# Two decode layers on one core: the last w2 in products of 512 columns, and x moved as its 16 real rows

## The chip, the cores and the metric

The kernel runs on one NeuronCore of a Trainium2 chip. The time is the device time of one execution in microseconds; the time before is the median of three runs. A profile is one more execution, taken by the hardware profiler.

## The reference

Two layers of the same weights, each a grouped-query attention with a cache and a gated feed-forward, for a batch of four single tokens. The part that matters:

```python
# B = 4, D = 512, 32 query heads, 8 kv heads, 4096 cached keys, Dh = 128, F = 1792, all float32
def _B_ref(x, w1, w3, w2):
    gate = jnp.einsum("bsd,df->bsf", x, w1)
    up = jnp.einsum("bsd,df->bsf", x, w3)
    h = _silu(gate) * up
    return jnp.einsum("bsf,fd->bsd", h, w2)

x = x + _A_ref(_layernorm(x), k_cache, v_cache, wq, wo)
x = x + _B_ref(_layernorm(x), w1, w3, w2)
# the same two lines once more: the second layer
```

The result is the last `x`, 4 rows of 512 numbers.

## The kernel before

**Loads.** All large arrays go through one buffer, `space`, of 216 units of 128 KB. The list `LOADS` names every load and its place, in the order in which they are issued on SyncE's queue. `pump` (L129 to L148) issues the next load as soon as its place is free in the program's order, and `done` (L153) frees a place after the last product that reads it and calls `pump` again. Before the first layer `x` is loaded on ScalarE's queue into `x_sb` (L161).

**The layout of x.** The 4 x 512 numbers stand in a 128 x 128 tile: column block k of 128 columns lies on partitions 32k to 32k+3, and the other 112 partitions are zeros. The host builds that tile for the input and takes the rows out of it for the output. `same` and the layer norm (`deviation`, `layernorm`) work on this layout.

**The accumulator bank.** `sums_ps` is one PSUM tile of 128 x 512. `x_ps` is its first 128 columns, `misc` its second 128, and `wide` all 512. The program is a tile framework's with a manual schedule: the order within each engine is the order of the code, and the framework puts in the semaphores.

**The feed-forward.** The w1 products (L473) fill `pg`; ScalarE takes the sigmoid (L478) and VectorE multiplies (L480). Then come the w3 products in two parts (`up`, L467), between them the residual: one product of the identity with `x_sb` starts the sum in `x_ps` (L517). `hidden` (L485) multiplies gate and up parts, `turn_h` turns the result into `hT`, in which chunk m of 128 hidden values is 128 partitions x 4 columns (L491, and L495 to L497 for the second part). `down` (L506 to L514) goes through the 14 chunks of w2: for each of the four column blocks k one product of `hT[:, m, :]` (the stationary side, 4 columns) with 128 columns of w2 is added to partitions 32k to 32k+3 of `x_ps`. After chunk 1 the second part of `hT` is turned.

In the last layer the w2 chunks come in five loads, of 4, 4, 3, 2 and 1 chunks. After the last chunk VectorE copies `x_ps` to `x_sb` (L579), and SyncE stores the 128 x 128 tile to `out` (L580).

Of the kernel before, what the change touches and what calls it, by code (L numbers as in the profile page):

```python
# [8 lines left out]
F32 = mybir.dt.float32  # L9
AF = mybir.ActivationFunctionType  # L10
# [3 lines left out]
B, D, HQ, HKV, SK, DH, F = 4, 512, 32, 8, 4096, 128, 1792  # L14
LAYERS = 2
REP = HQ // HKV
P = 128
KC = D // P
# [64 lines left out]
def tile_decode_layers(ctx: ExitStack, tc: tile.TileContext, x, kv, wqo, w1, w3, w2, out):  # L83
    nc = tc.nc
    ctx.enter_context(tc.manual_schedule())
    const = ctx.enter_context(tc.tile_pool(name="const", bufs=1))
    work = ctx.enter_context(tc.tile_pool(name="work", bufs=2))
# [5 lines left out]
    def place(at, n):  # L93
        return space[:, at * KB:(at + n) * KB]
# [34 lines left out]
    def pump():  # L129
        while state["next"] < len(LOADS):  # L130
            at, src, keys = entry(*LOADS[state["next"]])
            n = sum(size for _, size in keys)
            if any(taken[at:at + n]):
                return
            taken[at:at + n] = [True] * n
            dst = place(at, n)
            if src is None:
                for i in range(3):
                    nc.scalar.activation(dst[:, i * BLOCK:(i + 1) * BLOCK], stored[i], AF.Copy)
                nc.sync.dma_start(dst[:, 3 * BLOCK:], kv[TURN][:, 3 * BLOCK:2 * U])  # L140
            else:
                nc.sync.dma_start(dst, src)
            for key, size in keys:
                where[key] = at, size
                if key[:3] == ("kv", 0, TURN) and key[3] in KEPT:
                    where[("kv", 1, TURN, key[3])] = at, size
                at += size
            state["next"] += 1  # L148

    def loaded(*key):  # L150
        return place(*where[key])

    def done(layer, *key):  # L153
        if layer == 0 and (key[0] in ("wq", "wo") and key[1] >= HELD or key[:3] == ("kv", 0, TURN) and key[3] in KEPT):
            return
        at, n = where[key]
        taken[at:at + n] = [False] * n
        pump()

    x_sb = const.tile([P, P], F32, name="x_sb")  # L160
    nc.scalar.dma_start(x_sb, x)  # L161
    pump()


    ident = const.tile([P, P], F32, name="ident")
# [29 lines left out]
    hT = const.tile([P, 14, B], F32, name="hT")  # L195
    sums_ps = psum.tile([P, KC, P], F32, name="sums_ps")
    nc.vector.memset(sums_ps, 0.0)
    x_ps, misc = sums_ps[:, 0, :], sums_ps[:, 1, :]
    wide = sums_ps.rearrange("p k c -> p (k c)")
# [8 lines left out]
    def turned():  # L208
        return psum.tile([P, 4, P], F32, name="turned", tag="turned")


    def busy(n):
        if n:
            pt = scores().rearrange("p (k c) -> p k c", k=KC)
            nc.tensor.matmul(pt[:, 0:n, :], ident, ident.unsqueeze(1).to_broadcast([P, n, P]),
                             start=True, stop=True)
# [139 lines left out]
    def exponent(i, ps, acc, scale=None):  # L356
        p = work.tile([P, NT, P], F32, name="p", bufs=1)
        nc.scalar.activation(p.rearrange("p n s -> p (n s)"), ps, AF.Exp, bias=acc[:, i:i + 1],  # L358
                             scale=1.0 if scale is None else scale, accum_out=acc[:, 2 + i:3 + i])
        return p  # L360
# [97 lines left out]
    def feed_forward(layer, xT, rstd, factor):  # L458
        pg = o_ps[0]
        sides = o_ps[1], pg  # L460
        w1_sb = place(0, CORE).rearrange("p (k f) -> p k f", k=KC)

        def up(u, ks):
            for k in ks:
                w = loaded("w3", layer, KC * u + k)
                for j in range(4):
                    nc.tensor.matmul(sides[u][32 * j:32 * j + 32, 0:FW[u]], xT[:, 32 * k:32 * k + 32],  # L467
                                     w[:, j * FW[u]:(j + 1) * FW[u]], start=(k == 0), stop=(k == KC - 1))
                done(layer, "w3", layer, KC * u + k)

        for k in range(KC):
            for j in range(4):
                nc.tensor.matmul(pg[32 * j:32 * j + 32, 0:FJ], xT[:, 32 * k:32 * k + 32],  # L473
                                 w1_sb[:, k, j * FJ:(j + 1) * FJ], start=(k == 0), stop=(k == KC - 1))
            if k == 0:
                factor()
        gate = work.tile([P, FJ], F32, name="gate", tag="p", bufs=1)
        nc.scalar.activation(gate, pg[:, 0:FJ], AF.Sigmoid, scale=rstd[:, 0:1])  # L478
        nc.scalar.activation(spare, half[:, 0:1], AF.Exp)
        nc.vector.scalar_tensor_tensor(gate, pg[:, 0:FJ], rstd[:, 0:1], gate, op0=ALU.mult, op1=ALU.mult)  # L480
        pt = turned()

        def hidden(u):
            s = slice(FW[0] * u, FW[0] * u + FW[u])
            nc.vector.scalar_tensor_tensor(gate[:, s], sides[u][:, 0:FW[u]], rstd[:, 0:1], gate[:, s], op0=ALU.mult, op1=ALU.mult)  # L485

        def turn_h(u):
            if u == 0:
                busy(BUSY[3] if layer < LAYERS - 1 else 0)
                for i in range(2):  # L490
                    nc.tensor.transpose(pt[:, i, :], gate[:, i * P:(i + 1) * P], ident)  # L491
                nc.vector.tensor_copy(hT[:, 0:8, :],
                                      pt[:, 0:2, :].rearrange("p i (j b) -> p (i j) b", j=4)[:, :, 0:B])
            else:
                nc.tensor.transpose(pt[:, 2, :], gate[:, 2 * P:3 * P], ident)  # L495
                nc.tensor.transpose(pt[:, 3, :], gate[:, FJ - P:FJ], ident)
                nc.tensor.transpose(pt[0:64, 3, :], gate[:, FJ - 64:FJ], ident)  # L497
                nc.vector.tensor_copy(hT[:, 8:12, :],
                                      pt[:, 2, :].rearrange("p (j b) -> p j b", j=4)[:, :, 0:B])
                last = pt[:, 3, :].rearrange("p (j u b) -> p j u b", j=2, u=2)  # L500
                for i in range(2):
                    nc.vector.tensor_copy(hT[64 * i:64 * i + 64, 12:14, :],
                                          last[64 * i:64 * i + 64, :, i, 0:B])
            busy(BUSY[4] if layer < LAYERS - 1 else 0)

        def down():  # L506
            for m in range(14):
                t = loaded("w2", layer, m)
                for k in range(KC):
                    nc.tensor.matmul(x_ps[32 * k:32 * k + B, :], hT[:, m, :], t[:, k * P:(k + 1) * P],  # L510
                                     start=False, stop=(m == 13))
                done(layer, "w2", layer, m)
                if m == 1:
                    turn_h(1)  # L514

        up(0, range(KC))
        nc.tensor.matmul(x_ps, ident, x_sb, start=True, stop=False)  # L517
        hidden(0)
        up(1, (0, 1))
        turn_h(0)  # L520
        up(1, (2, 3))
        hidden(1)
        down()

    for layer in range(LAYERS):
# [14 lines left out]
        for n, (g, (first, last)) in enumerate(order):  # L540
# [6 lines left out]
            p = exponent(0, ps, acc, scale)  # L547
# [11 lines left out]
            p = exponent(1, ps, acc, scale)  # L559
# [16 lines left out]
        busy(BUSY[2])  # L576
        xT, rstd, factor = layernorm(rowsum)
        feed_forward(layer, xT, rstd, factor)
    nc.vector.tensor_copy(x_sb, x_ps)  # L579
    nc.sync.dma_start(out, x_sb)  # L580


# [43 lines left out]
```

## Time and profile before

| | |
|---|---|
| median of 3 runs | 705.6 us (705.35 to 705.66) |
| the profiled execution's own time | 705.49 us |
| its span | 703.7 us |
| TensorE busy (products) | 420.6 us, 60% |
| VectorE busy | 145.5 us, 21% |
| ScalarE busy | 41.8 us, 6% |
| data moved | 299.18 MB at a mean of 425 GB/s |
| w2 products, both layers (L510) | 224 records, 8.6 us busy |

The span runs from the first to the last instruction of the program; the execution's own time holds what lies around it as well. In the profile PE is TensorE's products and PEld its weight loads, DVE is VectorE, ACT ScalarE, POOL GpSimd, SP SyncE; a trailing q is the engine's instruction queue, which issues the loads. A row reads: line, engine, operation, result <- operands by the program's names, and the sizes as partitions x elements. An f32 product shows as two records, each with a weight load of its own.

### The profile page before, as it was taken

How to read it: one execution, taken by the hardware profiler on the slowest of the kernel's cores; microseconds unless marked ns; L12 is line 12 of the kernel's file. 1: busy time of each engine (PE TensorE's matmuls, PEld its weight loads, DVE VectorE, ACT ScalarE, POOL GpSimd, SP SyncE). 2: the span in 40 equal slices, each digit the busy share in tenths (PEclk: the TensorE clock that was granted, in tenths of full speed). 3: DMA queues.
4: the chain of work that ended last, by engine and by line, in shares of the span. 5: the costliest groups of instructions: out<-in, count | busy, mean ns of one | idle time of the engine just before them, and what ended most of it. 6: DMA issues, size and time to landing. Idle time of an engine off the chain costs nothing.

```text
span 703.7 us, 7223 instructions
## 1 busy us (share of the span) xinstructions
PE 420.6 (60%) x3162; PEld 131.4 (19%) x3162; DVE 145.5 (21%) x507; ACT 41.8 (6%) x99; POOL 3.1 (0%) x10
## 2 busy tenths in 40 slices
PE   2515634753765485486678984474554645656786
PEld 1101111211221121131124221121111211111223
DVE  3102102120130212232131322022111121212231
ACT  0000000100100000010111110010000001000011
POOL 0000000000000000000000000000000000000000
PEclk9967777875996787798899997697778878788889
DMA  9999999999999999999999999999999999999997
GB/s 417 421 414 423 465 421 425 420 460 422 416 456 427 419 443 447 402 432 430 421 416 390 422 446 433 440 418 427 449 443 426 418 434 443 428 429 421 425 420 295
DMA packets 12271, 299.18 MB, mean 425 GB/s; under 512 B 1360, under 2 KB 1616, under 8 KB 4048
## 3 DMA queue, kind: packets, MB, share of 16 engines
q1 hardware_dynamic: 12096, 298.65, 99.1%
q8 instruction: 25, 0.41, 0.2%
q10 hardware_dynamic: 144, 0.07, 0.0%
q14 instruction: 6, 0.05, 0.0%
HBM read 298.65 MB, written 0.07 MB: 424 GB/s over the span
## 4 chain that ended last, share of the span: by engine, by line
DMA 69%; PE 26%; another core or an unknown queue 2%; DVE 1%; ACT 1%; issue 1%; SPq 0%; ACTq 0%; DVEq 0%
DMA space<-in_kv 54%; PE scores L340 10%; PE o L401 10%; DMA space<-in_wqo 8%; DMA space<-in_w 6%; PE turned L365 1%; PE sums_ps L324 1%; ACT p L358 1%; DVE acc L352 1%; PE o L467 1%; PE stored L267 1%; PE stored L445 0%; DVE pT L367 0%; PE sums_ps L313 0%
## 5 line engine op out<-in xcount | busy, mean ns | idle before, releaser
L340 PE MATMUL scores<-space,qT 128*32 128x512 f32 x1024 | 166.0, 715 | 115.9 <-DMA space<-in_kv 115.4
L401 PE MATMUL o<-space,pT 128*16 128x512 f32 x1024 | 152.0, 726 | 112.2 <-DMA space<-in_kv 104.4
L401 PEld LDWEIGHTS o<-space,pT 128*16 128x16 f32 x1024 | 31.2, 110 | 216.7 <-DMA space<-in_kv 118.9
L340 PEld LDWEIGHTS scores<-space,qT 128*32 128x32 f32 x1024 | 35.0, 122 | 190.0 <-issue 185.3
L367 DVE COPY pT<-turned 128x256 f32<-128x256 f32 x32 | 13.6, 425 | 222.4 <-PE turned L365 222.4
L358 ACT ACTIVATE p<-scores,acc 128x512 f32<-128x512 f32 x30 | 20.6, 687 | 566.4 <-DVE acc L352 441.3
L352 DVE TENSOR_REDUCE acc<-scores 128x1 f32<-128x512 f32 x32 | 22.1, 691 | 122.3 <-PE scores L340 122.3
L414 DVE SCALAR_TENSOR_TENSOR o<-o,acc,o 128x128 f32<-128x128 f32 x112 | 39.3, 351 | 17.0 <-PE o L401 13.6
L313 PE MATMUL sums_ps<-space,xT 128*32 128x512 f32 x120 | 18.2, 684 | 20.8 <-DMA space<-in_wqo 20.8
L365 PE MATMUL turned<-ident,p 128*128 128x128 f32 x128 | 22.4, 300 | 12.7 <-ACT p L358 12.7
L425 DVE COPY oT<-sums_ps 128x16 f32<-128x16 f32 x16 | 2.8, 174 | 127.3 <-PE sums_ps L424 127.3
L365 PEld LDWEIGHTS turned<-ident,p 128*128 128x128 f32 x128 | 14.3, 148 | 44.4 <-ACT p L358 22.8
L324 PEld LDWEIGHTS sums_ps<-same,shares 128*128 128x128 f32 x120 | 15.9, 206 | 14.4 <-DVE shares L319 11.9
L324 PE MATMUL sums_ps<-same,shares 128*128 128x4 f32 x120 | 17.2, 266 | 1.0 <-DVE shares L319 1.0
L445 PE MATMUL stored<-space,oT 128*32 128x512 f32 x104 | 13.6, 596 | 0.0
L319 DVE TENSOR_SCALAR shares<-sums_ps,rstd 128x512 f32<-128x512 f32 x15 | 11.1, 743 | 1.8 <-PE sums_ps L313 1.8
L510 PE MATMUL sums_ps<-space,hT 128*4 128x128 f32 x224 | 8.6, 272 | 3.9 <-DMA space<-in_w 3.8
L424 PEld LDWEIGHTS sums_ps<-head,o 128*128 128x128 f32 x32 | 6.2, 242 | 22.1 <-issue 16.7
L467 PE MATMUL o<-space,xT 128*32 128x192 f32 (+1 forms) x128 | 8.7, 403 | 2.3 <-DMA space<-in_w 2.3
L313 PEld LDWEIGHTS sums_ps<-space,xT 128*32 128x32 f32 x120 | 3.3, 113 | 30.6 <-DMA space<-in_wqo 25.1
L424 PE MATMUL sums_ps<-head,o 128*128 128x16 f32 x32 | 7.8, 322 | 1.2 <-DVE o L414 1.2
L473 PE MATMUL o<-space,xT 128*32 128x448 f32 x64 | 6.8, 545 | 2.0 <-DMA space<-in_w 1.3
(102 smaller groups left out, 143.8 us busy)
## 6 DMA issues: line engine op xcount, KB each, us to landing
space<-in_kv SPq DMA_DIRECT2D x9, 4096.0 KB, 24.3
space<-in_wqo SPq DMA_DIRECT2D x4, 4096.0 KB, 29.9
space<-in_kv SPq DMA_DIRECT2D x2, 4608.0 KB, 19.8
space<-in_kv SPq DMA_DIRECT2D x3, 3072.0 KB, 28.4
space<-in_kv SPq DMA_DIRECT2D x8, 1024.0 KB, 8.7
space<-in_kv SPq DMA_DIRECT2D x1, 7168.0 KB, 29.1
space<-in_kv SPq DMA_DIRECT2D x1, 5632.0 KB, 22.9
space<-in_kv SPq DMA_DIRECT2D x3, 1536.0 KB, 12.2
```

What stands on the lines that cost most here:

```text
L313: nc.tensor.matmul(wide[32 * k:32 * k + 32, :], xT[:, 32 * k:32 * k + 32], w[:, k, :], start=True, stop=True)
L324: nc.tensor.matmul(misc[:, h * B:(h + 1) * B], shares[:, h * DH:(h + 1) * DH], same[:, 0:B], start=True, stop=True)
L340: nc.tensor.matmul(ps[32 * b:32 * b + 32, :], qT[:, b, at:at + 32], t[:, i * BLOCK:(i + 1) * BLOCK], start=(m < 2), stop=(m >= TILES - 2))
L352: nc.vector.tensor_reduce(acc[:, i:i + 1], ps, axis=AX.X, op=ALU.max, negate=True)
L358: nc.scalar.activation(p.rearrange("p n s -> p (n s)"), ps, AF.Exp, bias=acc[:, i:i + 1], scale=1.0 if scale is None else scale, accum_out ...
L365: nc.tensor.transpose(pt[:, n, :], p[:, n, :], ident)
L367: nc.vector.tensor_copy(pT, pt.rearrange("p n (b r) -> p n b r", b=B)[:, :, :, 0:ROW])
L401: nc.tensor.matmul(o_ps[i][32 * b:32 * b + ROW, :], pT[:, r // 2, b, :], t[:, j * NB * DH:(j + 1) * NB * DH], start=(r < 2), stop=(r >= TI ...
L414: nc.vector.scalar_tensor_tensor(o, o_ps[s][:, j * DH:(j + 1) * DH], acc[:, 16 + NB * s + j:17 + NB * s + j], o, op0=ALU.mult, op1=ALU.add)
L424: nc.tensor.matmul(misc[:, 0:B * REP], o, head, start=True, stop=True)
L445: nc.tensor.matmul(bank[32 * h:32 * h + 32, :], oT[:, h, :], w[:, h, :], start=first, stop=last)
L467: nc.tensor.matmul(sides[u][32 * j:32 * j + 32, 0:FW[u]], xT[:, 32 * k:32 * k + 32], w[:, j * FW[u]:(j + 1) * FW[u]], start=(k == 0), stop ...
```

## The change

In the last layer the w2 chunk is one product of all 512 columns, into partitions 0 to 3 of `wide`; the residual is brought there by four products with 4 columns of the identity each. The result then stands as 4 rows of 512. VectorE copies the first half of the columns and ScalarE the second half into a 4 x 512 tile `y`, which is stored as 4 rows of 2 KB. The first layer's `down` is as before. On the input side `x` comes as 4 x 512; `x_sb` is set to zero by VectorE and then filled by four loads of 4 rows each on ScalarE's queue.

```diff
     x_sb = const.tile([P, P], F32, name="x_sb")
-    nc.scalar.dma_start(x_sb, x)
+    nc.vector.memset(x_sb, 0.0)
+    for k in range(KC):
+        nc.scalar.dma_start(x_sb[32 * k:32 * k + B, :], x[:, k * P:(k + 1) * P])
     pump()
...
                 t = loaded("w2", layer, m)
-                for k in range(KC):
-                    nc.tensor.matmul(x_ps[32 * k:32 * k + B, :], hT[:, m, :], t[:, k * P:(k + 1) * P],
-                                     start=False, stop=(m == 13))
+                if layer == LAYERS - 1:
+                    nc.tensor.matmul(wide[0:B, :], hT[:, m, :], t, start=False, stop=(m == 13))
+                else:
+                    for k in range(KC):
+                        nc.tensor.matmul(x_ps[32 * k:32 * k + B, :], hT[:, m, :], t[:, k * P:(k + 1) * P],
+                                         start=False, stop=(m == 13))
                 done(layer, "w2", layer, m)
...
         up(0, range(KC))
-        nc.tensor.matmul(x_ps, ident, x_sb, start=True, stop=False)
+        if layer == LAYERS - 1:
+            for k in range(KC):
+                nc.tensor.matmul(wide[0:B, k * P:(k + 1) * P], ident[:, 32 * k:32 * k + B], x_sb, start=(k == 0), stop=False)
+        else:
+            nc.tensor.matmul(x_ps, ident, x_sb, start=True, stop=False)
         hidden(0)
...
-    nc.vector.tensor_copy(x_sb, x_ps)
-    nc.sync.dma_start(out, x_sb)
+    y = work.tile([B, D], F32, name="y", tag="p", bufs=1)
+    nc.vector.tensor_copy(y[:, 0:D // 2], wide[0:B, 0:D // 2])
+    nc.scalar.activation(y[:, D // 2:], wide[0:B, D // 2:], AF.Copy)
+    nc.sync.dma_start(out, y)
...
-        "x": rows.reshape(P, P),
+        "x": lay(x.reshape(B, D)),
...
-    args.append(nc.dram_tensor("out", (P, P), F32, kind="ExternalOutput").ap())
+    args.append(nc.dram_tensor("out", (B, D), F32, kind="ExternalOutput").ap())
```

More of the change, by code (lines that the diff above doesn't have):

```diff
@@ L593 @@
     w1, w3, w2 = np.asarray(B_w1), np.asarray(B_w3), np.asarray(B_w2)
-    rows = np.zeros((KC, 32, P), x.dtype)
-    rows[:, :B] = x.reshape(B, KC, P).transpose(1, 0, 2)
     def chunks(w):
@@ L623 @@
     r = run_bass_kernel_spmd(nc, [{f"in_{n}": a for n, a in arrays.items()}], core_ids=[0])
-    y = np.asarray(r.results[0]["out"]).reshape(KC, 32, P)[:, :B]
-    return np.ascontiguousarray(y.transpose(1, 0, 2)).reshape(B, 1, D)
+    return np.asarray(r.results[0]["out"]).reshape(B, 1, D)
```

## The prediction

> **What bounds the kernel now.** I read the page first, for its chain of work that ended last:
>
> ```profile
> DMA 69%; PE 26%; another core or an unknown queue 2%; DVE 1%; ACT 1%; issue 1%; SPq 0%; ACTq 0%; DVEq 0%
> ```
>
> So loads set most of the time. But an edit is paid where it stands, and this one stands at both ends of the program. The second view is therefore the chain in order of time (start, length, what), its last pieces:
>
> ```profile
> 684.84 14.83 DMA space<-in_w
> 699.71 0.62 PE sums_ps L510 x16
> 700.35 0.45 PE sums_ps L510 x8
> 700.82 0.29 DVE x_sb L579
> ```
>
> The last layer's w2 products (L510) end the kernel, and they are chained to the landing of w2, not to TensorE. The third view is the timeline of that stage (start, length, instruction, count, idle time before it):
>
> ```profile
> 692.07 0.49 PE L517 MATMUL sums_ps<-x_sb,ident 128*128 128x128 f32 x2
> ...
> 692.49 0.86 PE L467 MATMUL o<-space,xT 128*32 128x192 f32 x16
> ...
> 693.64 0.86 PE L467 MATMUL o<-space,xT 128*32 128x192 f32 x16
> ...
> 694.32 0.62 PE L510 MATMUL sums_ps<-space,hT 128*4 128x128 f32 x16
> 694.57 0.42 DVE L485 SCALAR_TENSOR_TENSOR gate<-o,rstd,gate 128x192 f32<-128x192 f32 x1 [0.63 <-PE o L467]
> ...
> 695.04 0.33 PE L495 MATMUL turned<-ident,gate 128*128 128x128 f32 x1
> ...
> 695.52 0.62 PE L510 MATMUL sums_ps<-space,hT 128*4 128x128 f32 x16
> ...
> 696.56 1.06 PE L510 MATMUL sums_ps<-space,hT 128*4 128x128 f32 x32 [0.42 <-DMA space<-in_w]
> ...
> 698.53 0.84 PE L510 MATMUL sums_ps<-space,hT 128*4 128x128 f32 x24 [0.91 <-DMA space<-in_w]
> ...
> 699.71 1.04 PE L510 MATMUL sums_ps<-space,hT 128*4 128x128 f32 x24 [0.34 <-DMA space<-in_w]
> ...
> 700.82 0.29 DVE L579 COPY x_sb<-sums_ps 128x128 f32<-128x128 f32 x1 [4.77 <-PE sums_ps L510]
> 701.14 0.35 SPq L580 DMA_DIRECT2D out<-x_sb  x1
> ```
>
> An f32 product is two records here: 14 chunks of w2, 4 column blocks each, 112 records. TensorE arrives at 694.32, runs to 696, and then waits three times for w2 (0.42, 0.91, 0.34 us). It runs each chunk as it lands.
>
> **The price of a product, packed and alone.** The four products of a chunk write partitions 0, 32, 64 and 96, so each uses its own quarter of the array's columns. Grouped by line (busy us, mean ns of one | idle before):
>
> ```profile
> L510 PE MATMUL sums_ps<-space,hT 128*4 128x128 f32 x224 | 8.6, 272 | 3.9 <-DMA space<-in_w 3.8
> L510 PEld LDWEIGHTS sums_ps<-space,hT 128*4 128x4 f32 x224 | 4.9, 85 | 7.1 <-DMA space<-in_w 4.1 <-issue 2.8
> L267 PE MATMUL stored<-space,columns 128*128 128x512 f32 x8 | 3.7, 605 | 0.0
> ```
>
> The 32 records at 696.56 take 1.06 us. Less the 0.27 of the last one, their starts spread over 0.79: eight sets of four, so 7 steps of 0.11 us. Four products of 128 columns thus cost two sets, 0.22 us a chunk. They run side by side; one after another they could not be 25 ns apart.
>
> After the change a chunk is one product of 512 columns with a 4-column stationary side, and every one goes to the same partitions 0 to 3, so nothing runs beside it. The trace has 512-column products in a row that share the array with nothing: L267. The weight loads of its later records start one record apart:
>
> ```profile
> 263.79 0.19 PEld L267 LDWEIGHTS stored<-space,columns 128*128 128x128 f32 x1 [0.24 <-issue]
> ...
> 265.93 0.19 PEld L267 LDWEIGHTS stored<-space,columns 128*128 128x128 f32 x1 [0.24 <-issue]
> ```
>
> Six loads, 2.14 us, so 0.428 us a record and 0.856 a product, with the load hidden. The stationary side there has 128 columns and not 4, but the time of a record follows the columns that stream: 0.428 is 3.9 times the 0.11 of 128. I take 0.856 a chunk where there was 0.22. The clock is no doubt of this row: it was 1.00 in the stage (columns: stretch, length, busy us of PE, PEld, DVE, ACT, POOL, granted clock, DMA share, GB/s):
>
> ```profile
> 694.00:697.40 3.40, 2.87 (x81) 1.92 (x71) 0.83 (x4) 0.00 (x0) 0.00 (x0) 1.00 0.97 392
> 697.40:700.80 3.40, 2.08 (x56) 1.01 (x48) 0.00 (x0) 0.00 (x0) 0.00 (x0) 1.00 0.37 146
> ```
>
> **The change part by part.**
>
> *The residual through the identity (L517).* One product of 128 columns becomes four, all in one column group: 4 x 2 x 0.107 (a quarter of 0.428) = 0.86 us. The old one held TensorE from 692.07 to 692.49, 0.42, of which 0.21 is its streaming; the rest I put down to the change between the 128-column and the 32-column form around it. The new form is that of its neighbours, so that part should go: +0.44, bounds +0.2 and +0.65. From there to 694.32 the records follow one another, so all of it is on the path. The first w2 product moves to 694.76.
>
> *The 14 chunks.* 28 x 0.428 = 11.98 us.
>
> *The transposes between chunk 1 and chunk 2.* They held TensorE from 695.04 to 695.52, 0.48, after waiting for the gate (L485, done at 694.99). Now two chunks last 1.7 us and the gate is ready before: 0.48 stays, its wait goes. Bounds: 0.33, three bare records, and 0.6 if a change of form ahead of them, which hid in the wait, now shows.
>
> The sum: 694.76 + 11.98 + 0.48 = 707.22; the last record ends 0.605 - 0.428 = 0.18 after its streaming: 707.40. The old end was 700.35 + 0.45 = 700.80, so +6.60. The w2 loads are no help or hindrance: chunks 4, 8 and 11 are reached at 698.7, 702.1 and 704.7, all after the old starts of 696.56, 698.53 and 699.71 that a landing had set. The three waits, 1.67 us in all, are filled, which is why the stage grows by less than 14 x 0.64 = 8.9.
>
> *Loads behind it.* Each chunk is handed back later, but nobody waits: the queue had issued its last load by 685.7.
>
> ```profile
> 673.36 12.28 SPq L142 DMA_DIRECT2D space<-in_w  x7
> ```
>
> *The copies.* One VectorE copy of 128 x 128 (0.29) becomes a VectorE copy of 4 x 256 and a ScalarE one of 4 x 256. I let the time follow the columns, not the rows. From the grouped rows: 0.43 for VectorE (L367). For ScalarE between 0.28 (128 columns) and 0.60 (512): 0.38.
>
> ```profile
> L367 DVE COPY pT<-turned 128x256 f32<-128x256 f32 x32 | 13.6, 425 | 222.4 <-PE turned L365 222.4
> L139 ACT ACTIVATE space<-stored 128x512 f32<-128x512 f32 x3 | 1.6, 598 | 0.5 <-PE sums_ps L279 0.5
> L275 ACT ACTIVATE x_sb<-sums_ps 128x128 f32<-128x128 f32 x1 | 0.3, 277 | 14.6 <-DVE xT L235 14.6
> ```
>
> Do they run side by side? The one place where both engines read one accumulator bank says no:
>
> ```profile
> 382.17 0.32 DVE L235 STREAM_TRANSPOSE xT<-sums_ps 128x128 f32<-128x128 f32 x1 [5.76 <-PE sums_ps L510]
> ...
> 382.52 0.28 ACT L275 ACTIVATE x_sb<-sums_ps 128x128 f32<-128x128 f32 x1 [14.60 <-DVE xT L235]
> ```
>
> ScalarE only reads what VectorE only reads, and starts 0.03 us after it is done. I take the copies one after the other: 0.43 + 0.03 + 0.38 + 0.03 = 0.87 from the first copy to the store, where 700.82 to 701.14 was 0.32: +0.55. Side by side it would be +0.14. The Trainium skill speaks against the split too: its page "PSUM — Partial Sum Buffer", section "PSUM bank collisions raise a hardware error", says that two engines on one bank and quadrant must be kept apart, two reads at disjoint columns as well. The row above shows equal columns only; by the rule the sum is 712.6, without it 712.2.
>
> *The store.* 8 KB in 4 rows in place of 64 KB in 128. The old one landed 1.6 us after its issue:
>
> ```profile
> out<-x_sb SPq DMA_DIRECT2D x1, 64.0 KB, 1.6
> x_sb<-in_x ACTq DMA_DIRECT2D x1, 64.0 KB, 5.3
> ```
>
> 64 KB at the page's mean of 425 GB/s is 0.15 us, so the rest is not bytes. Taken: 0; bounds -0.15, and +0.3 if fewer, longer rows use fewer of the DMA engines.
>
> *The start.* A memset on VectorE (128 x 128, some 0.2 us, in the time before 1.34 when VectorE is idle), then four loads of 16 rows in all, queued on ScalarE behind it:
>
> ```profile
> 0.73 0.40 ACTq L161 DMA_DIRECT2D x_sb<-in_x  x1
> ...
> 1.16 1.28 ACT L358 ACT_TABLE_LOAD   x1 [1.16 <-PEq L617]
> 1.34 1.19 DVE L169 TENSOR_REDUCE same<-ident 128x32 f32<-128x128 f32 x4 [1.34 <-POOL ident masks.py:199]
> ...
> 6.57 0.23 DVE L531 TENSOR_REDUCE rowsum<-x_sb 128x1 f32<-128x128 f32 x1
> ...
> 13.65 0.19 DVE L304 COPY qT<-sums_ps 128x32 f32<-128x32 f32 x1 [1.96 <-PE sums_ps L324]
> 1.16 24.11 DMA space<-in_kv
> 25.40 4.94 PE scores L340 x32
> 31.09 0.79 ACT p L358 x2
> ```
>
> If the four issues start at 1.0 and take 0.45 each, the last is out at 2.8; with the old 5.3 to landing x is there at 8.1, 1.5 us after L531 ran. The table load behind them on ScalarE's queue ends by 4.1 and is used at 31.09. What hides all of it: the query is ready at 13.84 and its first use, L340, waits for k until 25.40, 11.6 us later. Cost 0; without that cover 1.5 us. The 56 KB less are 0.13 us of load time, the lower bound.
>
> **Sum.** 6.60 + 0.55 = 7.15. The profiled execution took 705.49 us (span 703.7 and 1.8 around it); the median is 705.6, 0.1 away, which I leave out. 705.49 + 7.15 = 712.6.
>
> **Rivals.**
>
> *Weight loads no longer hide.* Now every load goes to the same four columns that the product before is still using. No row shows a run of loads into one group alone: L510's eight loads of a chunk rotate over four. If each of 28 loads (85 ns) stands bare, +2.4: 715.0. Against it: L267 reloads the whole array behind a running record. Chance 0.09.
>
> *A group alone is faster than one that shares.* If sharing slows the packed sets, a lone product costs less than four sets' worth, say three: 0.66, and 14 x 0.2 = 2.7 us go: 709.9. The Trainium skill's page "TensorE: Matmul & The Clock Gate", in "Part 3: Packing small matmuls — row/col tiling", measured 2.38 times for three column tiles and 3.07 for four row tiles, not 4. L267 against L510 gives 3.9. Chance 0.05.
>
> *The clock falls.* A stream that fills 4 of 128 columns might be granted half the clock. If it falls from chunk 2 on: 24 x 0.428 = 10.3 more, 722.9. Against it: 1.00 in the stage, although TensorE waited there. Chance 0.03.
>
> *Not slower: w2's landing still ends the stage.* This decides if a lone product costs at most 0.39 us: chunks 0 to 12 (13 x 0.39, and 0.48 of transposes, from 694.76) are then done by 700.35, when the old last chunk started, and one product is left, ending at 700.35 + 0.39 + 0.18 = 700.92, +0.12. With the copies side by side (+0.14) that is 705.7, and with the store's -0.15 and x's -0.13 it is 705.5. It needs half of L267's price. Chance 0.04.
>
> **How the numbers follow.** Forecast 0.78, at 712.6. Its own bounds: 711.5 (identity 0.24 less, transposes 0.15, copies 0.41, store 0.15, x 0.13) to 713.3 (0.21, 0.12 and 0.3 more). The range reaches on to the bare weight loads and the 0.2 above them, 711.5 to 715.2, and leaves out the half clock, the three-sets case and the hidden stage, 0.12, and a little of the rest. 0.2% is 1.4 us, somewhat more than a measurement of this kernel needs to tell from no change. Slower by over 0.2%: 0.95; within: 0.04; faster: 0.01, kept for a gain that none of these cases gives.
>
> **What would show it.** L510 in the last layer: 28 records of 128x512, starts 0.43 apart, no idle put down to in_w after the first chunk, ending near 707.4; L517 four products in about 0.9 us; ScalarE's copy starting after VectorE's has ended; the store issued near 708.3; L340 still first released by k near 25.3. Starts 0.51 apart would show bare loads, about 0.33 the second rival; waits on in_w up to 700.3 the last. Wrong altogether would be a span under 709 or over 716.

## The result, and the profile after

The changed kernel takes 711.8 us (711.42 to 712.01) where the kernel before, run in turn with it, takes 706.06: a ratio of 1.0076, interval 1.0061 to 1.009. It is slower. The forecast was 712.6 in a range of 711.5 to 715.2, so the time itself lies inside. The difference does not: +7.1 us was forecast, the range began at +5.9 (711.5 less the 705.6 it was built on), and the medians of the sets differ by +5.2 to +5.8; the interval of the first set, +4.3 to +6.4, still reaches into it. Two more sets of the same pair: 1.0077 (1.0061 to 1.0093) and 1.008 (1.0067 to 1.0093).

The profiled execution after took 712.0 us, its span 710.2, against 705.49 and 703.7. The end of its chain in order of time (start, length, what):

```profile
694.53 1.70 PE sums_ps L512 x4
...
696.71 10.41 PE sums_ps L512 x24
707.12 0.02 issue
707.14 0.42 DVE y L589
707.56 0.02 issue
707.59 0.37 ACT y L590
```

The landing of w2, which stood here for 14.83 us, is gone. TensorE's own stream ends the kernel, then two copies in a row. The timeline of the stage (L512 is the w2 product now, L524 the identity, L469 the w3 products):

```profile
689.97 1.91 PE L469 MATMUL o<-space,xT 128*32 128x256 f32 x32
...
691.69 0.93 PE L524 MATMUL sums_ps<-x_sb,ident 128*4 128x128 f32 x7
...
692.46 0.27 PE L524 MATMUL sums_ps<-x_sb,ident 128*4 128x128 f32 x1
...
694.35 1.88 PE L512 MATMUL sums_ps<-space,hT 128*4 128x512 f32 x4
...
696.16 0.33 PE L497 MATMUL turned<-ident,gate 128*128 128x128 f32 x1
...
696.64 10.46 PE L512 MATMUL sums_ps<-space,hT 128*4 128x512 f32 x24
...
697.07 0.09 PEld L512 LDWEIGHTS sums_ps<-space,hT 128*4 128x4 f32 x1 [0.34 <-issue]
...
706.08 0.09 PEld L512 LDWEIGHTS sums_ps<-space,hT 128*4 128x4 f32 x1 [0.34 <-issue]
707.14 0.41 DVE L589 COPY y<-sums_ps 4x256 f32<-4x256 f32 x1 [9.97 <-PE sums_ps L512]
707.59 0.37 ACT L590 ACTIVATE y<-sums_ps 4x256 f32<-4x256 f32 x1 [15.14 <-DVE y L589]
707.98 0.35 SPq L591 DMA_DIRECT2D out<-y  x1
```

No product waits for w2 any more. From the third weight load of the long run (697.07) to the last there are 21 steps in 9.01 us, 0.429 each: the 0.428 of the forecast's row, with the load of the next weights hidden. The two copies follow one another, and ScalarE's wait is put down to VectorE's copy. And at the start something the forecast did not have (the same view, first 28 us):

```profile
1.03 1.72 ACTq L163 DMA_DIRECT2D x_sb<-in_x  x4
...
5.60 0.33 SPq L142 DMA_DIRECT2D space<-in_kv  x1
...
20.08 0.28 DVE L540 TENSOR_REDUCE rowsum<-x_sb 128x1 f32<-128x128 f32 x1 [13.42 <-DMA x_sb<-in_x]
...
27.22 0.19 DVE L306 COPY qT<-sums_ps 128x32 f32<-128x32 f32 x1 [1.96 <-PE sums_ps L326]
27.46 5.36 PE L342 MATMUL scores<-space,qT 128*32 128x512 f32 x32 [0.28 <-DVE qT L306]
```

x is complete at 20 us, not at 8. The query is ready at 27.4, and the first scores now wait for it, 2.1 us after the 25.40 at which k had released them.

### The profile page after: what moved, and what is told of

It is laid out like the page before. It is cut to its first block, busy times and chain, and to the rows that moved or that the text cites. A ratio compares the mean times of both kernels' runs of the same rounds, so it can differ in the third digit from the quotient of the medians.

```text
span 710.2 us, 7076 instructions
## 1 busy us (share of the span) xinstructions
PE 428.3 (60%) x3084; PEld 131.8 (19%) x3084; DVE 145.9 (21%) x508; ACT 42.2 (6%) x100; POOL 3.0 (0%) x10
## 4 chain that ended last, share of the span: by engine, by line
DMA 70%; PE 27%; DVE 1%; ACT 1%; issue 1%; SPq 0%; ACTq 0%; DVEq 0%
DMA space<-in_kv 57%; PE o L403 10%; DMA space<-in_wqo 9%; PE scores L342 9%; DMA space<-in_w 4%; PE sums_ps L512 2%; PE turned L367 1%; PE sums_ps L326 1%; PE o L469 1%; ACT p L360 1%; PE stored L269 1%; DVE acc L354 0%; PE stored L447 0%; PE o L475 0%; DVE pT L369 0%
## 5 line engine op out<-in xcount | busy, mean ns | idle before, releaser
L225 PE MATMUL o<-rowsum,same 128*128 128x1 f32 x8 | 1.6, 275 | 20.4 <-DVE rowsum L540 20.4
L512 PE MATMUL sums_ps<-space,hT 128*4 128x512 f32 x28 | 12.3, 592 | 0.0
```

Of the source, the lines that this page charges most:

```text
L512: nc.tensor.matmul(wide[0:B, :], hT[:, m, :], t, start=False, stop=(m == 13))
```

## The experiments

**What makes the w2 stage long.** Theory: a product that nothing runs beside pays its whole stream of 512 columns. Rival: the width or the full bank costs more, wherever the product goes.

*Chunks rotate over the four column groups:*

```diff
-                    nc.tensor.matmul(wide[0:B, :], hT[:, m, :], t, start=False, stop=(m == 13))
+                    q = 32 * (m % 4)
+                    nc.tensor.matmul(wide[q:q + B, :], hT[:, m, :], t, start=(0 < m < 4), stop=(m >= 10))
```

> The changed kernel with chunk m going to partitions 32*(m mod 4), so that following products of 512 columns use different column groups; the sum of the four parts is left out. Theory (what is lost is that nothing runs beside a product): chunks run side by side again and wait for w2 again; the last one starts at about 700.3, ends at 701.3, the store goes out near 702.2 and the time is 706.2. Rival (a product of 512 columns costs more for its width or its full bank, wherever it goes): records stay 0.43 apart and the time stays at 711.8.

Measured: 706.1 us (705.74 to 708.12), ratio to the kernel before 1.0002 (0.9991 to 1.0013). Its timeline:

```profile
695.34 1.91 PE L513 MATMUL sums_ps<-space,hT 128*4 128x512 f32 x12
...
698.15 2.83 PE L513 MATMUL sums_ps<-space,hT 128*4 128x512 f32 x12 [0.91 <-DMA space<-in_w]
...
699.97 0.09 PEld L513 LDWEIGHTS sums_ps<-space,hT 128*4 128x4 f32 x2 [0.55 <-DMA space<-in_w]
701.02 0.41 DVE L590 COPY y<-sums_ps 4x256 f32<-4x256 f32 x1 [5.16 <-PE sums_ps L513]
701.47 0.37 ACT L591 ACTIVATE y<-sums_ps 4x256 f32<-4x256 f32 x1 [9.47 <-DVE y L590]
```

Products of the same shape, the same number of records, the same copies: twelve records now take 1.91 us where they took about 5.3 (12 x 0.429 and the end of the last one), and the stage waits for w2 again. Within that interval the whole cost was the one column group. The rotation also gives each product another place to add to. That this is not what helps shows in the run with two banks below: there the products of one group alternate between two accumulators, and 512 columns still take 0.86 us.

*Two groups of 256 columns:*

```diff
-                    nc.tensor.matmul(wide[0:B, :], hT[:, m, :], t, start=False, stop=(m == 13))
+                    for j in range(2):
+                        nc.tensor.matmul(wide[32 * j:32 * j + B, 0:256], hT[:, m, :], t[:, 256 * j:256 * j + 256],
+                                         start=False, stop=(m == 13))
```

> The changed kernel with two column groups in place of one: per chunk two products of 256 columns, into partitions 0 and 32, side by side; one VectorE copy of 256 columns, two stores. Theory (the price is what streams through one group): a chunk costs 2 x 0.214 = 0.43 us in place of 0.86; from 694.0 the 14 chunks and 0.57 of transposes end at about 700.6, nearly as w2 lands (700.2), so the copy starts near 700.9 and the time is 705.0 to 705.8, against 711.8 with one group. Rival (any move away from four packed products of 128 columns costs the same 6 us): 711 to 712.

Measured: 706.04 us (705.72 to 708.65), ratio 1.001 (1.0 to 1.0019). The step from one group to two takes back nearly all of the 6 us. The profiled execution was one in which all loads came later (the last load of wq and wo is issued at 674.92 us, 672.89 in the kernel before), but the length of the stream is read there:

```profile
697.65 2.85 PE L513 MATMUL sums_ps<-space,hT 128*4 128x256 f32 x24
...
701.05 2.76 PE L513 MATMUL sums_ps<-space,hT 128*4 128x256 f32 x24 [0.54 <-DMA space<-in_w]
```

Six chunks in 2.85 us, 0.45 a chunk after the last record's tail is taken off, as forecast; the median is 0.2 us above the top of the expected 705.0 to 705.8. 0.43 us a chunk is what w2's landing leaves time for, 0.86 is not.

**The two halves of the change.**

> The changed kernel with the old load of x (128 rows of 512 B). Theory A: the whole cost is here and 0.1 to 0.3 us on top of the changed kernel, 711.9 to 712.2; the chain to the first w2 product about 0.27 later. Rival (chance): equal to the changed kernel, 711.4 to 712.0.

Measured, with the w2 and store edits and the old load of x: 712.74 us (711.84 to 713.63), ratio 1.009 (1.0072 to 1.0108). The cost is all here. The median of these four runs lies above both expectations and 0.9 us above the changed kernel of the same set, which is not explained.

> The kernel before with the x edit alone: zeroed tile and four loads of 4 rows; w2 and the store as before. Theory A: everything up to the last layer's w2 runs 0.1 to 0.3 us earlier, as in the profile of the changed kernel (L467 at 689.97 in place of 690.23), so 705.2 to 705.5. Rival (the 0.26 us is chance of the load stream): no shift that repeats, 705.5. Neither expects a cost: the query's first use waits for k until about 25.3 us in both.

Measured, with the x edit alone: 705.29 us (704.92 to 707.17) against 706.57, ratio 0.9983 (0.9968 to 0.9998). Below the kernel before by more than the 0.13 us of its bytes, in a set in which the kernel before ran high. Three kernels were to tell what in the edit that could be:

```diff
+    # the edit's number of loads, the old bytes
+    for k in range(KC):
+        nc.scalar.dma_start(x_sb[32 * k:32 * k + 32, :], x[32 * k:32 * k + 32, :])
...
+    # the edit's bytes in one load of 16 rows, spread by one product
+    nc.scalar.dma_start(x16, x)
+    nc.tensor.matmul(x_ps, spread, x16, start=True, stop=True)
+    nc.vector.tensor_copy(x_sb, x_ps)
```

> The kernel before with x in four loads of 32 full rows each (64 KB in all, behind the same memset as in the x edit): the number of loads of the edit with the bytes of before. In two sets the kernels with the x edit had medians 0.9 to 1.3 us below their partners with the old load, more than the 0.13 us of its bytes. Theory S (fewer bytes and packets beside the first loads): no gain, median near that of the kernel before, 706.0 to 706.6. Theory Q (three more loads, so that the fifth large load is issued at 5.6 and not 2.8 us): the gain is here, median 705.2 to 705.6. Theory N (chance between sets of runs): both x kernels of this call lie within 0.3 us of the kernel before.

> The kernel before with x in one load of its 16 rows (8 KB), spread to the 128 x 128 tile by one product with a selection matrix at the start: the bytes of the edit with the number of loads of before. The query is ready some 1 us later, hidden until k lands at about 25.3. Theory S: median 705.2 to 705.6. Theory Q: no gain, 706.0 to 706.6. Theory N: within 0.3 us of the kernel before.

> The x edit alone once more, beside the two variants. Theories S and Q: median 705.2 to 705.6, 0.6 to 1.0 below the kernel before. Theory N: within 0.3 us of it.

Measured beside a kernel before at 705.78: four full loads 705.96 (1.0001, 0.9993 to 1.001), one load of 16 rows 705.57 (0.9997, 0.9988 to 1.0005), the edit again 705.59 (1.0, 0.9991 to 1.0008). All within 0.3 us: theory N, although the last two also lie in the microseconds that S and Q gave, since the kernel before ran lower here than in the sets those were worked out from. The gain of the first set did not repeat and is not shown to be the edit's; one of 0.1 to 0.2 us is neither shown nor excluded. What these profiles do show is the price of a load in the queue. Four full loads:

```profile
x_sb<-in_x ACTq DMA_DIRECT2D x4, 16.0 KB, 15.7
...
26.39 0.29 DVE L533 TENSOR_REDUCE rowsum<-x_sb 128x1 f32<-128x128 f32 x1 [19.73 <-DMA x_sb<-in_x]
...
33.77 2.79 PE L342 MATMUL scores<-space,qT 128*32 128x512 f32 x12 [0.28 <-DVE qT L306]
```

One load of 16 rows:

```profile
x<-in_x ACTq DMA_DIRECT2D x1, 8.0 KB, 3.2
...
25.23 2.79 PE L347 MATMUL scores<-space,qT 128*32 128x512 f32 x12 [10.03 <-DMA space<-in_kv]
```

One load beside the large ones lands in 3.2 us (5.3 with 64 KB). Four in one queue are complete much later, at 20 us with 8 KB and at 26.4 with 64 KB; the four of 16 KB each landed between 4.6 and 23.7 us after their issue, so one after the other. The Trainium skill, "DMA: Bandwidth & Descriptors", section "Queues, rings and completion order", says that each DMA engine takes turns between the queues by packets. By that, a small load that must wait out a large packet of the other queue for each turn would look like this, but no run here changed the packets. Even 8.4 us of delay at the first scores (33.77 against 25.40) cost nothing that the sets can tell.

**The copies.** Theory: the common accumulator bank keeps the engines apart.

```diff
+                    for bank, j in ((wide, 0), (stored[2], 1)):
+                        nc.tensor.matmul(bank[0:B, 0:256], hT[:, m, :], t[:, 256 * j:256 * j + 256], ...)
+    nc.scalar.activation(y[:, D // 2:], stored[2][0:B, 0:D // 2], AF.Copy)
```

> The changed kernel with the two halves of the columns summed in two accumulator banks (products of 256 columns, two per chunk, still in partitions 0 to 3), so that VectorE and ScalarE copy from different banks. Theory (the copies run one after the other because they share a bank): ScalarE's copy starts with VectorE's, the store goes out 0.40 to 0.45 us earlier after the last product, 711.4 where the changed kernel has 711.8; the stream of products keeps its length, 14 x 4 x 0.214 = 12.0 us. Rival (the framework orders them for the common tile y, not for the bank): still one after the other, 711.8.

Measured: 711.53 us (711.12 to 712.21), ratio 1.0077 (1.0063 to 1.0091).

```profile
705.88 0.59 PE L513 MATMUL sums_ps<-space,hT 128*4 128x256 f32 x2
...
706.31 0.59 PE L513 MATMUL stored<-space,hT 128*4 128x256 f32 x2
706.51 0.41 DVE L592 COPY y<-sums_ps 4x256 f32<-4x256 f32 x1 [9.60 <-PE sums_ps L513]
706.94 0.37 ACT L593 ACTIVATE y<-stored 4x256 f32<-4x256 f32 x1 [14.76 <-DVE y L592]
707.34 0.35 SPq L594 DMA_DIRECT2D out<-y  x1
```

The store went out 0.44 us after the last product's end (706.90) in place of 0.88, as early as the theory had it, but by another way: VectorE copied its bank while TensorE finished the other. ScalarE's start falls together with the end of its own last product and of VectorE's copy, so it proves nothing. Two tiles for the copies, one bank:

```diff
-    y = work.tile([B, D], F32, name="y", tag="p", bufs=1)
+    y = work.tile([B, D // 2], F32, name="y", tag="p", bufs=1)
+    z = work.tile([B, P], F32, name="z", tag="tmp", bufs=1)
```

> The changed kernel with the two copies going to two tiles of their own (one bank is still the source of both; ScalarE copies 128 columns, which are stored twice, so the last quarter of the result is left out). In the run with two banks ScalarE's start fell together with the end of its own last product and with the end of VectorE's copy, so it told nothing. Theory (the common bank orders them): ScalarE still starts when VectorE's copy has ended, 0.43 us after it started. Rival (the common tile y orders them): both start within 0.05 us of each other.

```profile
707.66 0.41 DVE L590 COPY y<-sums_ps 4x256 f32<-4x256 f32 x1 [9.97 <-PE sums_ps L512]
708.10 0.35 SPq L592 DMA_DIRECT2D out<-y  x1
708.10 0.27 ACT L591 ACTIVATE z<-sums_ps 4x128 f32<-4x128 f32 x1 [15.14 <-DVE y L590]
```

ScalarE still starts 0.44 us after VectorE, with no result tile in common. That is the theory. Bank and source tile are one and the same in this program, so a rule by tile is not told from one by bank. The rule of the Trainium skill's page "PSUM — Partial Sum Buffer", section "PSUM bank collisions raise a hardware error", is kept here for disjoint columns too, as an order in the program. The one run, with its three stores, took 712.63 us. And one copy in place of two:

> The changed kernel with one VectorE copy of all 512 columns and no ScalarE copy. If the two copies gain nothing from each other, one copy costs what VectorE's 512-column reads of this bank cost, 0.69 us, where the two in a row take 0.84: the store 0.15 us earlier after the last product, 711.6 against 711.8. If they had run side by side, one copy would be 0.26 slower than the pair, 712.0.

```profile
707.01 0.68 DVE L589 COPY y<-sums_ps 4x512 f32<-4x512 f32 x1 [9.97 <-PE sums_ps L512]
707.72 0.35 SPq L590 DMA_DIRECT2D out<-y  x1
```

0.71 us from copy to store where the pair took 0.84; 711.62 us (711.34 to 711.89), as expected, though 0.2 us is inside the interval of the runs. The split over two engines costs a little and gains nothing.

**The store and the x edit with the packed products.**

```diff
+    for k in range(KC):
+        (nc.sync, nc.scalar)[k % 2].dma_start(out[:, k * P:(k + 1) * P], x_sb[32 * k:32 * k + B, :])
```

> The kernel before with the x edit, the packed w2 products kept, and the result stored as its 16 real rows by four stores of 4 rows of 512 B (two on SyncE's queue, two on ScalarE's). Theory A (the ends give 0.3 us at the start and 0.35 at the store): 704.8 to 705.2. Rival (the store's gain was the single store's four long rows, and four stores pay issue one after the other): 705.2 to 705.6. If the x edit also calms the runs, they spread over less than 0.5 us where those of before spread over 2 to 5; if the spread comes from the landing of the last w2 loads, it stays.

Measured: 705.82 us (705.56 to 706.65), ratio 0.9995 (0.9986 to 1.0004): no gain that can be told, above the ranges of both theory A (to 705.2) and its rival (to 705.6).

```profile
700.70 0.29 DVE L581 COPY x_sb<-sums_ps 128x128 f32<-128x128 f32 x1 [5.25 <-PE sums_ps L512]
701.01 0.66 SPq L583 DMA_DIRECT2D out<-x_sb  x2
701.02 0.62 ACTq L583 DMA_DIRECT2D out<-x_sb  x2
```

From 701.01 to the span's end at 703.9 are 2.9 us, where the single store of 64 KB left 2.6 (701.14 to 703.7) and that of 8 KB 2.2 (707.98 to 710.2). So the gain belongs to one store of four rows, and four stores give it back.

**Why the sets differ by less than the profiles.**

> The changed kernel once more, timed in turn with the kernel before. The forecast was +7.1 us, the first comparison gave 711.8 against 706.06 with the runs of before spread over 705.35 to 708.37. Theory A (the ends were mis-sized): its profile ended 6.5 us later than the one of before, so the difference is 6.3 to 6.6 whenever the kernel before runs at 705.4. Theory B (the runs of before drift): the changed kernel stays at 711.4 to 712.0 and the difference is 4 to 6, set by where the runs of before fall. In the profile: L512 starts 0.43 apart, ScalarE's copy after VectorE's.

> The changed kernel in one more set beside the kernel before. The profiles differ by 6.5 us, the sets so far by 5.2 to 5.7, and the kernel before had medians of 706.06, 706.57, 706.04 and 705.78. If the gap to the profiles is the drift of the kernel before from set to set, the changed kernel stays at 711.6 to 711.9 and the difference is 711.8 less the median of before in this set. If the changed kernel takes part in the drift, it moves with the set and the difference stays at 5.2 to 5.7.

Measured: 711.82 us against 706.57, and 711.81 (711.41 to 712.92) against 706.0. The changed kernel has medians of 711.8, 711.82 and 711.81; the kernel before 706.06, 706.57, 706.04, 705.78 and 706.0. That is theory B, and the drift of the kernel before in the last expectation: the difference is set by where the kernel before falls. The later sets ran on four different chips, so a drift in time and a difference between chips are not told apart. Its profile (705.49) and the first three runs (705.35 to 705.66) were at its low end. Does the scatter sit in the landing of the last w2 loads, which the long w2 stage would cover?

```diff
         hidden(1)
+        if layer == LAYERS - 1:
+            for _ in range(7):
+                busy(4)
         down()
```

> The kernel before with seven idle products of 512 columns (6.0 us) ahead of the last layer's w2 products, so that all w2 has landed when they start; x as before. Theory D (the runs of before spread by the landing of the last w2 loads): w2 starts at 700.3, the 14 chunks take 3.1 us and 0.5 for the transposes, the copy starts near 704.1 and the time is 708.7 to 708.9, with all runs within 0.4. Theory C (the spread comes with the old load of x, or from the streams ahead of the last layer): the same time at best, but runs spread over 1 us or more.

> The same seven idle products with x loaded as its 16 rows. Theory D: 708.4 to 708.7, spread as small as that of the other late tail. Theory C: 0.2 to 0.4 us below the other at its best and within 0.4 us, while the other spreads over 1 us or more.

The timeline with the old x:

```profile
691.10 1.91 PE L467 MATMUL o<-space,xT 128*32 128x256 f32 x32
...
695.30 8.23 PE L215 MATMUL scores<-ident 128*128 128x512 f32 x14
...
696.48 0.30 PEld L215 LDWEIGHTS scores<-ident 128*128 128x128 f32 x2 [0.89 <-PE scores L215]
...
703.45 0.62 PE L510 MATMUL sums_ps<-space,hT 128*4 128x128 f32 x16
...
704.48 2.80 PE L510 MATMUL sums_ps<-space,hT 128*4 128x128 f32 x96
```

The idle products took 8.2 us and not 6.0, since the weights of each were loaded only when the products of the one before were done (0.89 us of waiting); with these 2.2 the forecast is 711, and the medians are 710.73 and 710.28. The runs: 710.71, 710.73, 710.73, 710.88 and 712.02 with the old x, 710.12, 710.22, 710.28, 711.7 and 711.72 with the new. Most lie close, as theory D wants, but three of ten are 1.3 to 1.5 us higher. Both kept traces are of such high runs (712.02 and 711.7), and no product waits for w2 in them. They are late already where the w3 products of the last layer begin. The kernel before, and the late tail with the new x:

```profile
690.23 1.91 PE L467 MATMUL o<-space,xT 128*32 128x256 f32 x32
...
690.89 1.91 PE L469 MATMUL o<-space,xT 128*32 128x256 f32 x32
```

With the old x it is 691.10, 0.9 us after the kernel before. With the new x it is 690.89, where the two profiles of the x edit alone have 689.37 and 689.78. So by these comparisons most of the 1.3 to 1.5 us was lost ahead of those products, where the second half of theory C had put it. What loses it there stays open; neither the late w2 nor the load of x explains all of the scatter.

## Why the forecast was right and wrong

*Direction and mechanism: right, and shown.* The lone column group turns a stage that w2's landing ended into one that TensorE ends. The steps of 0.429 (0.428 in the sum) and the rotating chunks leave no other place for the cost. Of the rivals, bare weight loads would have shown steps of 0.51, three sets' worth 0.33, a falling clock steps of 0.86, and w2's landing waits to the end: none is there, and the granted clock was 1.00 from 694 to 706.5 us.

*The terms.* The profiles differ by 6.5 us, 0.65 less than the 7.15 of the sum. The transposes took 0.57 (0.48), from 694.35 + 4 x 0.429 to 696.64. The copies took 0.84 (0.87). The identity cost 0.3 (0.44): the w3 products before it began 0.26 earlier and the w2 products 0.03 later than before. That 0.26 itself was not in the sum: 0.13 of it is, by the prediction's estimate, the bytes that x saves; the rest is inside the scatter, since two more profiles of the changed kernel have this start at 689.66 and 689.96 and the one with the old x at 690.07. The store, taken at 0 with a bound of 0.15, gave 0.33: from its issue to the end of the execution's own time 705.49 - 701.14 = 4.35 before, 712.0 - 707.98 = 4.02 after. No run separates its bytes from its rows.

*The step that failed* is the one that looked safest: "the median is 705.6, 0.1 away, which I leave out". The range had a width for its terms and none for the kernel before. All 88 runs of the kernel before have a median of 706.0 and a middle half from 705.66 to 706.62; those of the changed kernel, 16 in all, a median of 711.8 with 15 between 711.41 and 712.17. So the profile of before stood 0.5 under its kernel and that of after 0.2 over: 6.5 - 0.7 = 5.8, just under the +5.9 at which the range began. It took both errors: the terms alone give 6.5 and this step alone 7.15 - 0.7 = 6.45, and both of these lie inside. Why the kernel before scatters stays open.

*The start: right in its cost, wrong in its reason.* x was to land at 8.1 and landed at 20; the 11.6 us of cover were used up and 2.1 more. I had given all four loads one landing time, although each stands behind the one ahead of it in its queue. What hid it in fact was the load stream: the chain of the trace goes through a large load that was issued at 5.60 us and landed at 53.1, and the first scores had freed the next place by 41.1, where it was 38.5 before and 48.4 with the four full loads.

## What to carry to other kernels

Small products that fill a quarter of the array's columns are cheap only while three others run beside them (0.22 us a chunk here, 0.86 without); merging four of them into one wide product saves instructions and multiplies the stream by four, which decides as soon as the stage had been fed by loads just fast enough. Price a change to such a stage at the point where the last load lands: two groups (0.43 us a chunk) still fit, one (0.86) does not. And before a forecast of 1%, ask how far one profile and three runs can stand from the kernel's median; here it was half a microsecond, as large as any term but the first.

## What was not expected of the hardware

Four small loads in one queue beside large loads of another took 19 us for 8 KB, a single one of the same bytes 3.2. Two copies out of one bank on two engines took 0.84 us, one copy on one engine 0.71, from its start to the store. The scatter of the kernel before, up to 710.47 us, has no cause shown here; in the two late runs that were traced, most of the delay was there before the last layer's w3 products.
